# Four whole row tiles in float32, x for two row tiles per step with half-height low terms, and a new order list

## The chip, the core and the metric

The kernel runs on one core of one Trainium2 chip. The metric is the device time of one execution in microseconds (us). The core has five engines with queues of their own that work through their instructions strictly in program order: TensorE (PE, matmuls; PEld is its weight load), VectorE (DVE), ScalarE (ACT), GpSimd (POOL) and SyncE (SP), which issues the DMAs. An instruction that waits holds up everything behind it on its own engine.

## The reference

Linear attention, followed by a two-layer block with a softmax-gated activation:

```python
q_s = softmax(q, over head_dim);  k_s = softmax(k, over the sequence)
kv  = einsum('bhsd,bhse->bhde', k_s, v)          # 8 batches, 8 heads, seq 576, head_dim 64
x   = einsum('bhsd,bhde->bhse', q_s, kv)         # as 4608 rows of 512
h   = x @ w_in                                   # 512 -> 1024
solu = h * softmax(h, over the 1024)
out = ((solu - mean) / sqrt(var + 1e-6) * g_ln) @ w_out      # 1024 -> 512
```

All inputs and outputs are float32; q is drawn with a spread of 0.8.

## The kernel before

The 4608 rows are 36 row tiles of 128. A batch b has four tiles (b, 0) to (b, 3); the 64 rows that are left of two neighbouring batches make one further tile (b, 4) of the odd batch, the "rest tile". For each tile there are three works: x (attention product, transposed), h (the first big matmul with the activation behind it) and o (the second big matmul and the store). Besides there are K and V (per batch: keys, values, the kv product), Q and R (softmax of q and its transpose, R for the rest tiles), S (scales), w and y (weights from HBM), W and Z (weights scaled into float16 pairs) and P (four idle matmuls on the zeroed tile bd2).

Float32 products are made in float16 as high and low parts. For h, each tile takes 24 matmuls of 128x128 by 512 columns (L605); for o, 24 more (L679). For x (`attend`, L573), a head's kv is a block of 64 columns, and rows 0 to 63 and 64 to 127 hold the high and the low part of q: one matmul of all 128 rows with kv-high in both halves, one with kv-low above zeros. Two heads write the two column halves of a result at the same time, so these matmuls are 128 rows by 64 columns. One tile takes 16 of them at 128 columns; a rest tile takes 32 at 64 columns, 16 per batch.

The first tiles are done in float32 ("whole", WHOLE = 2 tiles): q is transposed on PE (`whole_queries`, L511), x is made by `attend_whole` (L551) and h by eight float32 matmuls (L597) with the unscaled weights iw. Their order of weight blocks is FIRST = 3, 0, 2, 1. Whole tiles need neither the float16 weights wi nor the float16 kv (tile bd).

Buffers matter in three places. PSUM holds two h results, one o result (a second kind of bank is used for some of the last six tiles), and three banks with the tag "att" that x, kv and the small transposes share. An h result is freed by the Square on ACT (L648) and the low part of u on DVE (L641); an o result by its copy-out, os, on ACT (L689) or DVE (L687).

The order of all of this is written out by hand in the string ORDER: each word names a work, and each occurrence runs that work's generator to its next `yield`. `.v` puts the step on DVE, and no suffix leaves it on its default engine. So ORDER decides what stands behind what on every engine.

Instance names below: h1_1 is the h of batch 1, tile 1; o0_00 is the o of tile (0, 0); os0_00 is its copy-out; e0_3 and u0_3 belong to h0_3; wo is the scaled second weight; gw its unscaled source.

Of the kernel before, what the change touches and what calls it, by code (L numbers as in the profile page):

```python
# [8 lines left out]
F32 = mybir.dt.float32  # L9
# [8 lines left out]
P = 128  # L18

BUFS = 12, 4, 2  # L20
FIRST = 3, 0, 2, 1
WHOLE = 2
ORDER = (
# [76 lines left out]
def linear_attention_solu_ffn(ctx: ExitStack, tc: tile.TileContext, q, k, v, w_in, w_out, g_ln, out):  # L100
# [13 lines left out]
    C = 4  # L114
# [27 lines left out]
    for t in reversed(bd):  # L142
        nc.gpsimd.memset(t, 0.0)
# [291 lines left out]
    def q_softmax(x, parts, n, name, place=None):  # L435
# [30 lines left out]
        if place is not None:  # L466
            return
# [331 lines left out]
```

## Time and profile before

| what | value |
|---|---|
| runs | 468.74, 468.83, 471.92 us |
| median | 468.83 us |
| profiled execution | 472.39 us, of which 470.6 us from first to last instruction |
| PE busy | 443.1 us, 94% |
| DVE busy | 336.1 us, 71% |
| ACT busy | 280.1 us, 60% |
| POOL busy | 212.3 us, 45% |
| mean granted TensorE clock | 0.985 |

The three runs fall apart into two near 468.8 us and one at 471.92 us; the profiled execution lies beside the upper one. TensorE's clock was at its full level (2.4 GHz) but for a few stretches at the lower one (1.2 GHz).

A timeline row reads: start, duration, engine, line, operation, output and inputs, shape, count, and in brackets the idle time of the engine before it with what ended it. A row of merged matmuls counts from the start of the first to the end of the last, and ends overlap with the next start; so the distance between two starts is the better measure of what a stretch cost.

### The profile page before, as it was taken

What the parts mean: (1) busy time and instruction counts of PE and PEld (TensorE: products, weight loads), DVE (VectorE), ACT (ScalarE), POOL (GpSimd) and SP (SyncE); (2) the same over time, 40 slices, a digit from 0 to 9 for tenths busy, and PEclk for the clock granted to TensorE, in tenths of its full rate; (3) what the DMA queues carried; (4) which work ended last, traced back from release to release, by engine and by line L of the source; (5) the groups of instructions that cost most, each with busy time, mean ns of one, the idle gap of its engine ahead of it and who ended that gap; (6) DMA issues with size and microseconds to landing.
All of it is one profiled execution on the core that took longest, in us unless ns stands there. A gap on an engine that the chain in (4) does not pass through costs nothing.

```text
span 470.6 us, 9239 instructions
## 1 busy us (share of the span) xinstructions
PE 443.1 (94%) x3619; PEld 218.2 (46%) x3619; DVE 336.1 (71%) x598; ACT 280.1 (60%) x469; POOL 212.3 (45%) x312
## 2 busy tenths in 40 slices
PE   3579989799999999999999999999999999999996
PEld 0334434255455454544454455444545454444444
DVE  4978999969878897987788857869567654434411
ACT  2858999658458775764765865434766472433320
POOL 3113876547467555832573584233334631212100
PEclk9969999899999999999999999999999999999999
DMA  8889768368976957497876872986422744431432
GB/s 286 289 293 259 194 163 237 71 156 177 240 210 142 232 121 194 118 275 138 221 174 131 205 167 54 229 205 136 116 68 55 118 100 88 68 91 58 99 91 68
DMA packets 139468, 74.53 MB, mean 158 GB/s; under 512 B 116248, under 2 KB 124704, under 8 KB 139424
## 3 DMA queue, kind: packets, MB, share of 16 engines
q1 hardware_dynamic: 139424, 73.94, 63.9%
q8 instruction: 28, 0.46, 0.4%
q14 instruction: 16, 0.13, 0.1%
HBM read 36.70 MB, written 9.44 MB: 98 GB/s over the span
## 4 chain that ended last, share of the span: by engine, by line
PE 83%; DVE 7%; ACT 4%; DMA 3%; issue 2%; SPq 0%; ACTq 0%; DVEq 0%
PE o L679 39%; PE h L605 34%; PE x L573 3%; PE kv L397 3%; PE h L597 2%; DMA w_in<-in_moe_w_in_dram 2%; DMA km<-in_k_dram 1%; DVE top L612 1%; DVE h L634 1%; ACT wo L335 1%; DVE qsum L454 1%; DVE gw L263 1%; DVE qnmx L447 0%; DVE u L641 0%; ACT gw L259 0%
## 5 line engine op out<-in xcount | busy, mean ns | idle before, releaser
L679 PE MATMUL o<-wo,uT 128*128 128x512 f16 (+1 forms) x888 | 199.1, 376 | 3.0 <-ACT os L689 3.0
L605 PE MATMUL h<-wi,xT 128*128 128x512 f16 x816 | 187.9, 379 | 1.6 <-ACT e L648 1.6
L679 PEld LDWEIGHTS <-uT 128*128 128x128 f16 x888 | 86.5, 98 | 101.2 <-issue 5.8
L605 PEld LDWEIGHTS <-xT 128*128 128x128 f16 x816 | 79.1, 98 | 94.3 <-issue 2.1
L612 DVE TENSOR_REDUCE top<-h 128x1 f32<-128x1024 f32 x36 | 43.8, 1218 | 30.9 <-PE h L605 30.1
L641 DVE SCALAR_TENSOR_TENSOR u<-h,nmu,u 128x1024 f16<-128x1024 f32 x36 | 45.9, 1275 | 17.1 <-ACT u L639 16.9
L634 DVE SCALAR_TENSOR_TENSOR h<-h,ph,e 128x1024 f32<-128x1024 f32 x36 | 46.2, 1284 | 10.3 <-POOL ph L631 7.2
L648 ACT ACTIVATE e<-h,nmu 128x1024 f32<-128x1024 f32 x36 | 40.0, 1110 | 17.5 <-DVE u L641 17.3
L628 POOL TENSOR_TENSOR p<-pi,mone 128x1 f32<-128x1 f32 x36 | 23.9, 665 | 45.9 <-DVE pi L625 43.8
L614 ACT ACTIVATE nm<-top,hs 128x1 f32<-128x1 f32 x30 | 8.8, 294 | 56.7 <-DVE top L612 56.7
L639 ACT ACTIVATE u<-h,nmu 128x1024 f16<-128x1024 f32 x36 | 40.0, 1111 | 0.9
L461 POOL TENSOR_TENSOR qm<-qm,qrec 128x1024 f32<-128x1024 f32 x14 | 26.6, 1902 | 24.8 <-DVE qrec L458 13.6
L618 ACT ACTIVATE e<-h,nm,hs 128x1024 f32<-128x1024 f32 x30 | 36.0, 1201 | 0.7
L689 ACT ACTIVATE os<-o,rr 128x512 f32<-128x512 f32 (+1 forms) x25 | 16.8, 674 | 30.0 <-PE o L679 23.4
L383 POOL TENSOR_TENSOR km<-km,kb 128x1152 f32<-128x1152 f32 x11 | 29.0, 2641 | 7.1 <-ACT kb L361 7.1
L471 POOL TENSOR_TENSOR qhl<-qm,qhl 128x1024 f16<-128x1024 f32 x10 | 21.3, 2130 | 23.5 <-ACT qhl L160 13.5
L636 ACT ACTIVATE nmu<-s 128x1 f32<-128x1 f32 x36 | 7.3, 203 | 41.1 <-DVE h L634 39.0
L622 POOL TENSOR_SCALAR am<-nm 128x1 f32<-128x1 f32 x22 | 10.2, 462 | 45.7 <-ACT nm L614 45.6
L449 POOL TENSOR_TENSOR qm<-qm,qnmx 128x1024 f32<-128x1024 f32 (+1 forms) x15 | 26.8, 1786 | 8.6 <-DVE qnmx L447 8.5
L661 POOL TENSOR_TENSOR r<-var,mhalf 128x1 f32<-128x1 f32 x36 | 19.7, 552 | 23.5 <-DVE var L658 21.4
L582 DVE SCALAR_TENSOR_TENSOR xT<-x,xT 128x512 f16<-128x512 f32 x34 | 22.8, 679 | 8.6 <-ACT xT L580 8.6
L580 ACT ACTIVATE xT<-x 128x512 f16<-128x512 f32 x34 | 19.4, 591 | 7.6 <-PE x L573 7.6
(147 smaller groups left out, 536.9 us busy)
## 6 DMA issues: line engine op xcount, KB each, us to landing
v<-in_v_dram SPq DMA_DIRECT2D x32, 288.0 KB, 4.1
km<-in_k_dram SPq DMA_DIRECT2D x7, 1152.0 KB, 6.9
out_dram<-os SPq DMA_DIRECT2D x31, 256.0 KB, 2.9
qm<-in_q_dram SPq DMA_DIRECT2D x7, 1024.0 KB, 6.1
w_in<-in_moe_w_in_dram SPq DMA_DIRECT2D x8, 512.0 KB, 8.2
w_out<-in_moe_w_out_dram SPq DMA_DIRECT2D x8, 512.0 KB, 6.1
out_dram<-os SPq DMA_DIRECT2D x10, 128.0 KB, 2.4
km<-in_k_dram SPq DMA_DIRECT2D x2, 576.0 KB, 6.7
```

The source lines that it names most:

```text
L383: on(nc.gpsimd).tensor_tensor(km[:, ns], km[:, ns], wide, op=ALU.subtract)
L449: on(nc.gpsimd).tensor_tensor(x, x, wide(nmx), op=ALU.add)
L461: on(nc.gpsimd).tensor_tensor(x, x, wide(rec), op=ALU.mult)
L605: nc.tensor.matmul(h[:, ns], xT[:, t, kc], wi[:, s, kc, ns], start=(i == 0), stop=(i == len(terms) - 1))
L612: nc.vector.tensor_reduce(top, h, axis=AX.X, op=ALU.max, negate=True)
L618: nc.scalar.activation(e, h, AF.Exp, bias=nm, scale=hs, accum_out=z)
L628: nc.gpsimd.tensor_tensor(p, pi, mone, op=ALU.pow)
L634: nc.vector.scalar_tensor_tensor(h, h, ph, e, op0=ALU.mult, op1=ALU.mult, accum_out=s1)
L639: nc.scalar.activation(u[:, 0], h, AF.Identity, bias=nmu)
L641: nc.vector.scalar_tensor_tensor(u[:, 1], h, nmu, u[:, 0], op0=ALU.add, op1=ALU.subtract)
L648: nc.scalar.activation(e, h, AF.Square, bias=nmu, accum_out=s2)
L679: nc.tensor.matmul(o, uT[:, j, f], wo[:, s, f, cols], start=(f == 0 and j == 0 and s == 0), stop=(f == NF - 1 and j == 1))
```

## The change

Whole tiles. WHOLE goes from 2 to 4, so all four full tiles of batch 0 run in float32 from q to h. `whole_queries` now takes a range of tiles: tiles 2 and 3 share one softmax, and each has its own transposes on PE. Their DMA transpose and their split into high and low parts are gone.

x for two tiles. From batch 1 on, one x step makes a pair of tiles, so its matmuls have 256 columns. For the upper four heads the places of q's high and low part are swapped. The low part of kv then meets q's high part in rows 0 to 63 for heads 0 to 3 and in rows 64 to 127 for heads 4 to 7, so the low matmuls have 64 rows by 64 columns and the zero halves fall away, with two of the three memsets. The result of a pair lies in two PSUM banks, each copied out on its own. Rest tiles go through the same code with 64 columns.

```diff
-BUFS = 12, 4, 2
+BUFS = 12, 3, 2
-WHOLE = 2
+WHOLE = 4
 ORDER = (
-    "LQ0*2 Q0b LK0 LG Q0c.v V00 K0 Q0c.v LK0 K0 K0.v w3 K0 w3 LG P K0 V02.v Q0b Q0c LG K0 Q0b V00 w0 "
+    "LQ0*2 LK0 Q0a*2 Q0c LK0 K0.v Q0c.v K0 w3 K0.v K0 Q0b Q0a.v w3 K0 V02 Q0a Q0b K0.v Q0a.v Q0c V00 K0.v "
...
-    for t in reversed(bd):
-        nc.gpsimd.memset(t, 0.0)
+    nc.gpsimd.memset(bd[2], 0.0)
...
-                places[0:D, 1, :, i], kvn[hp], s[hp], high[hp], op0=ALU.mult, op1=ALU.subtract
+                places[hp, 1, :, i], kvn[hp], s[hp], high[hp], op0=ALU.mult, op1=ALU.subtract
...
+        parts = [(x[:, hs], hi, lo) for hs, hi, lo in parts()]
+        for y, hi, lo in parts:
+            cast(on(nc.scalar), hi, y)
+        yield
+        for y, hi, lo in parts:
+            on(nc.gpsimd).tensor_tensor(lo, y, hi, op=ALU.subtract)
...
-    def attend(row_tile):
+    def attend(row_tiles):
...
-            for pr in range(NP):
-                for s in range(2):
-                    for j in range(2):
-                        nc.tensor.matmul(
-                            acc[j * D : (j + 1) * D, pr, cols], t[:, s, 2 * pr + j], qT[:, 2 * pr + j, cols],
-                            start=(s == 0), stop=(s == 1),
-                        )
+            for s, g, i in turns:
+                rows = slice(g * D, (g + 1) * D) if s else slice(0, P)
+                for j in range(2):
+                    head = g * H // 2 + 2 * i + j
+                    nc.tensor.matmul(
+                        accs[g][j * D : (j + 1) * D, i, :, cols], t[rows, s, head], qT[rows, :, head, cols],
+                        start=(m == s == i == 0), stop=(m + 1 == len(groups) and s == 1 and 2 * i + 2 == NP),
+                    )
...
-        nc.scalar.activation(xT[:, 0], acc, AF.Copy, scale=1.0 / QS)
-        yield
-        nc.vector.scalar_tensor_tensor(xT[:, 1], acc, 1.0 / QS, xT[:, 0], op0=ALU.mult, op1=ALU.subtract)
-        yield
+        for acc, ns in zip(accs, halves):
+            nc.scalar.activation(xT[:, 0, ns], acc, AF.Copy, scale=1.0 / QS)
+            yield
+            nc.vector.scalar_tensor_tensor(xT[:, 1, ns], acc, 1.0 / QS, xT[:, 0, ns], op0=ALU.mult, op1=ALU.subtract)
+            yield
...
-        works[f"Q{b}c"] = queries(b, 2, 4)
+        works[f"Q{b}c"] = whole_queries(b, 2, 4) if (b, 3) in whole else queries(b, 2, 4)
```

ORDER is a new list throughout. Three places of it are shown. The first is PE where the first o result ends and the next one begins. Before, o0_10 follows o0_00 directly:

```order
L679 MATMUL o0_00_947<-wo_68,uT0_0_538 128x512
L679 LDWEIGHTS uT0_1_729
L679 MATMUL o0_10_1021<-wo_68,uT0_1_729 128x512
L679 LDWEIGHTS uT0_1_729
L679 MATMUL o0_10_1021<-wo_68,uT0_1_729 128x512
```

In the change the last third of h1_1 stands there (eight matmuls in all), and o0_10 comes after it:

```order
L694 MATMUL o0_00_863<-wo_68,uT0_0_527 128x512
L620 LDWEIGHTS xT1_0_814
L620 MATMUL h1_1_841<-wi_67,xT1_0_814 128x512
L620 LDWEIGHTS xT1_0_814
L620 MATMUL h1_1_841<-wi_67,xT1_0_814 128x512
```

The 24 matmuls of h1_1 stood ahead of o0_00 as one block; in the change they are three blocks of eight, ahead of, inside and behind o0_00.

The second place is ACT at the copy-out of the first o result. Before, from the last scaled weights on:

```order
L335 ACTIVATE wo_68<-gw3_750,gs_882 128x512 x2
L618 ACTIVATE e0_3_954,z0_3_955<-h0_3_771,nm0_3_896,hs0_456 128x1024
L451 ACTIVATE qm1_446<-qm1_446 128x8x128
L451 ACTIVATE qr0_450<-qr0_450 128x512
L636 ACTIVATE nmu0_3_986<-s10_3_984 128x1
L160 COPY vm_78<-v2_0_799 128x9x64
L639 ACTIVATE u0_3_990<-h0_3_771,nmu0_3_986 128x1024
L614 ACTIVATE nm1_1_1008<-top1_1_1006,hs1_805 128x1
L689 ACTIVATE os0_00_1014<-o0_00_947,rr0_0_941 128x512
```

In the change:

```order
L335 ACTIVATE wo_68<-gw3_567,gs_783 128x512 x2
L451 ACTIVATE qm1_485<-qm1_485 128x8x128
L633 ACTIVATE e0_3_871,z0_3_872<-h0_3_729,nm0_3_832,one_75 128x1024
L704 ACTIVATE os0_00_917<-o0_00_863,rr0_0_816 128x512
L651 ACTIVATE nmu0_3_923<-s10_3_921 128x1
L654 ACTIVATE u0_3_925<-h0_3_729,nmu0_3_923 128x1024
```

The copy-out moved from behind nm1_1, u0_3 and nmu0_3 to right behind e0_3.

The third place is ACT around the Square (s2) of tile (0, 2), which frees the PSUM room of h1_1. Before:

```order
L636 ACTIVATE nmu0_2_783<-s10_2_781 128x1
L639 ACTIVATE u0_2_786<-h0_2_610,nmu0_2_783 128x1024
L313 ACTIVATE junk_out3_810,gw_sum_94<-gw3_750 128x1024
L580 ACTIVATE xT1_1_860<-x1_1_826 128x512
L648 ACTIVATE e0_2_721,s20_2_873<-h0_2_610,nmu0_2_783 128x1024
L580 ACTIVATE xT1_0_884<-x1_0_843 128x512
L335 ACTIVATE wo_68<-gw0_428,gs_882 128x512
```

In the change:

```order
L654 ACTIVATE u0_2_766<-h0_2_552,nmu0_2_753 128x1024
L428 COPY bd1_81<-bd1_81 64x256
L335 ACTIVATE wo_68<-gw0_445,gs_783 128x512
L335 ACTIVATE wo_68<-gw0_445,gs_783 128x512
L595 ACTIVATE xT1_0_814<-x1_0_0_787 128x512
L663 ACTIVATE e0_2_709,s20_2_822<-h0_2_552,nmu0_2_753 128x1024
L595 ACTIVATE xT1_0_814<-x1_0_1_788 128x512
```

Two of the eight scalings of wo moved ahead of that Square, and the last of the weight sums (junk_out) lies further ahead than the rows shown.

## Rows read from the trace of the kernel before

**Rows 1.** The page's first part: busy time, share of span, instructions.

```profile
PE 443.1 (94%) x3619; PEld 218.2 (46%) x3619; DVE 336.1 (71%) x598; ACT 280.1 (60%) x469; POOL 212.3 (45%) x312
```

**Rows 2.** Windows: stretch, its length, PE, PEld, DVE, ACT, POOL busy, clock, DMA.

```profile
80.00:90.00 10.00, 7.01 (x29) 2.79 (x26) 9.71 (x16) 8.82 (x16) 3.10 (x5) 0.88 0.22 65
90.00:100.00 10.00, 10.00 (x45) 4.45 (x44) 5.40 (x13) 3.16 (x5) 4.60 (x5) 0.95 0.93 216
...
40.00:90.00 50.00, 43.50 (x359) 20.43 (x357) 47.51 (x79) 46.71 (x78) 33.04 (x39) 0.98 0.69 178
90.00:460.00 370.00, 369.02 (x2986) 181.32 (x2985) 258.87 (x457) 209.75 (x357) 168.45 (x259) 1.00 0.63 144
```

**Rows 3.** Chain that ended last, in order of time: start, us, what.

```profile
37.25 5.17 PE h L597 x12
...
438.41 28.57 PE o L679 x156
```

**Rows 4.** Timeline of PE, 60 to 95 us.

```profile
74.05 5.34 PE L605 MATMUL h<-wi,xT 128*128 128x512 f16 x24 [0.29 <-ACT e L648]
79.23 5.34 PE L679 MATMUL o<-wo,uT 128*128 128x512 f16 x24
87.56 7.03 PE L679 MATMUL o<-wo,uT 128*128 128x512 f16 x24 [2.98 <-ACT os L689]
```

**Rows 5.** Timeline of ACT, 60 to 95 us.

```profile
72.80 1.11 ACT L648 ACTIVATE e<-h,nmu 128x1024 f32<-128x1024 f32 x1
...
78.83 2.56 ACT L335 ACTIVATE wo<-gw,gs 128x512 f16<-128x512 f32 x4
81.29 1.19 ACT L618 ACTIVATE e<-h,nm,hs 128x1024 f32<-128x1024 f32 x1
...
86.63 0.29 ACT L614 ACTIVATE nm<-top,hs 128x1 f32<-128x1 f32 x1 [0.87 <-DVE top L612]
86.83 0.67 ACT L689 ACTIVATE os<-o,rr 128x512 f32<-128x512 f32 x1
```

**Rows 6.** Lines by form: xcount, busy us, mean ns, idle before.

```profile
L597 PE MATMUL h<-iw,xT 128*128 128x512 f32 x32 | 15.5, 632 | 0.0
...
L580 ACT ACTIVATE xT<-x 128x512 f16<-128x512 f32 x34 | 19.4, 591 | 7.6 <-PE x L573 7.6
L160 ACT CAST qhl<-qm 128x1024 f16<-128x1024 f32 x8 | 8.3, 1036 | 1.1 <-POOL qm L461 1.1
L160 ACT COPY qT<-qt 128x512 f32<-128x512 f32 x2 | 1.1, 564 | 0.0
L166 ACT ACTIVATE xT<-x 128x256 f32<-128x256 f32 x2 | 0.7, 374 | 0.0
```

**Rows 7.** Timeline of PE, 24 to 60 us, at the first scale.

```profile
34.07 3.08 PE L597 MATMUL h<-iw,xT 128*128 128x512 f32 x4
36.98 0.27 PE L172 MATMUL wide_in<-ident,m_in 128*128 128x128 f32 x1
```

**Rows 8.** Timeline of ACT, 24 to 48 us, the scale's first use.

```profile
38.19 2.19 ACT L288 ACTIVATE wi<-iw,s_in 128x1024 f16<-128x1024 f32 x2 [1.25 <-DVE isc L285]
```

**Rows 9.** Timelines of PE at three x steps.

```profile
128.43 1.08 PE L573 MATMUL x<-qT,bd 128*64 128x128 f16 x32
129.34 0.67 PE L573 MATMUL x<-qTr,bd 128*64 128x64 f16 x32
129.95 0.60 PE L679 MATMUL o<-wo,uT 128*128 128x512 f16 x2
...
184.85 1.08 PE L573 MATMUL x<-qT,bd 128*64 128x128 f16 x32
185.87 0.82 PE L679 MATMUL o<-wo,uT 128*128 128x512 f16 x3
...
290.06 0.70 PE L573 MATMUL x<-qTr,bd 128*64 128x64 f16 x32
290.69 2.03 PE L397 MATMUL kv<-vm,km 64*64 64x65 f32 x122
```

More of the change, by code (lines that the diff above doesn't have):

```diff
@@ L459, in q_softmax @@
         yield
-        if place is None:
-            on(nc.gpsimd).tensor_tensor(x, x, wide(rec), op=ALU.mult)
-        else:
-            y, z = (a.rearrange("p (i n) d -> p i n d", i=2) for a in (x, wide(rec)))
-            on(nc.gpsimd).tensor_tensor(place, y, z, op=ALU.mult)
+        if places is not None:
+            for i, place in enumerate(places):
+                y, z = (a if len(shape) == 3 else a[:, :, i] for a in (x, wide(rec)))
+                y, z, place = (a.rearrange(e + " d -> p i n d", i=2) for a, e in ((y, "p (i n)"), (z, "p (i n)"), (place, "p (n i)")))
+                on(nc.gpsimd).tensor_tensor(place, y, z, op=ALU.mult)
+                yield
+            return
+        on(nc.gpsimd).tensor_tensor(x, x, wide(rec), op=ALU.mult)
         yield
-        if place is not None:
-            return
-        hi, lo = parts()
-        cast(on(nc.scalar), hi, x)
+        parts = [(x[:, hs], hi, lo) for hs, hi, lo in parts()]
+        for y, hi, lo in parts:
+            cast(on(nc.scalar), hi, y)
         yield
-        on(nc.gpsimd).tensor_tensor(lo, x, hi, op=ALU.subtract)
+        for y, hi, lo in parts:
+            on(nc.gpsimd).tensor_tensor(lo, y, hi, op=ALU.subtract)
         yield
     qT_of, hl_of = {}, {}
+    QUARTERS = slice(0, H // 2), slice(H // 2, H)
     def queries(b, c0, c1):
@@ L485, in parts @@
             hl = hl_of[b, c0 // 2]
-            if n == 1:
-                return (hl[:, c0 % 2, :, i] for i in range(2))
-            return (hl[:, :, :, i].rearrange("p c h d -> p h c d") for i in range(2))
+            for g, hs in enumerate(QUARTERS):
+                if n == 1:
+                    yield hs, *(hl[:, c0 % 2, hs, i ^ g] for i in range(2))
+                else:
+                    yield hs, *(hl[:, :, hs, i ^ g].rearrange("p c h d -> p h c d") for i in range(2))
         yield from q_softmax(x[:, :, 0] if n == 1 else x, parts, H * n, f"{b}_{c0}")
@@ L498, in queries, with whole_queries @@
         )
-    def whole_queries(b, c):
-        first = c // 2 * 2
+    def whole_queries(b, c0, c1):
+        first = c0 // 2 * 2
         if ("whole", first) not in hl_of:
             hl_of["whole", first] = sb.tile([P, 2, H, D], F32, name=f"qn{b}_{first}", tag="qhl", bufs=1)
-        qn = hl_of["whole", first][:, c % 2]
-        place = qn.rearrange("p (n i) d -> p i n d", i=2)
-        yield from q_softmax(raw["qm"][:, :, c], None, H, f"{b}_{c}", place)
-        flat = qn.rearrange("p h d -> p (h d)")
-        turned = ps.tile([P, NP, P], F32, name=f"qt{b}_{c}", tag="att", bufs=3)
-        for i in range(NP):
-            nc.tensor.transpose(turned[:, i], flat[:, i * P : (i + 1) * P], ident)
-        yield
-        if (b, c) not in qT_of:
-            t = sb.tile([P, 2, NP, P], F32, name=f"qT{b}_{first}", tag="qT", bufs=2)
-            qT_of.update({(b, k): t for k in (first, first + 1) if (b, k) in whole})
-        cast(on(nc.scalar), qT_of[b, c][:, c % 2], turned)
+        cs = range(c0, c1)
+        qn = [hl_of["whole", first][:, c % 2] for c in cs]
+        x = raw["qm"][:, :, c0:c1]
+        yield from q_softmax(x[:, :, 0] if len(cs) == 1 else x, None, H * len(cs), f"{b}_{c0}", qn)
+        for c, y in zip(cs, qn):
+            flat = y.rearrange("p h d -> p (h d)")
+            turned = ps.tile([P, NP, P], F32, name=f"qt{b}_{c}", tag="att", bufs=3)
+            for i in range(NP):
+                nc.tensor.transpose(turned[:, i], flat[:, i * P : (i + 1) * P], ident)
+            yield
+            if (b, c) not in qT_of:
+                t = sb.tile([P, 2, NP, P], F32, name=f"qT{b}_{first}", tag="qT", bufs=2)
+                qT_of.update({(b, k): t for k in (first, first + 1) if (b, k) in whole})
+            cast(on(nc.scalar), qT_of[b, c][:, c % 2], turned)
+            yield
     def rest_queries(b):
@@ L520, in parts @@
             hl_of["rest"] = sb.tile([P, H, 2, D], F16, name=f"qhlr{b}", tag="qhlr", bufs=1)
-            return (hl_of["rest"][:, :, i] for i in range(2))
+            for g, hs in enumerate(QUARTERS):
+                yield hs, *(hl_of["rest"][:, hs, i ^ g] for i in range(2))
         yield from q_softmax(raw["qr"], parts, H, f"r{b}")
@@ L556, in attend_whole @@
             yield
-    def attend(row_tile):
-        b, c = row_tile
+    def attend(row_tiles):
+        (b, c), n = row_tiles[0], len(row_tiles)
         name = f"{b}_{c}"
         if c < C:
-            groups = [(b, qT_of[b, c][:, c % 2], slice(0, P))]
+            groups = [(b, qT_of[b, c][:, c % 2 : c % 2 + n], slice(0, P))]
         else:
-            groups = [(b - 1 + j, qT_of["rest", b // 2], slice(j * R, (j + 1) * R)) for j in range(2)]
-        acc = ps.tile([P, NP, P], F32, name=f"x{name}", tag="att", bufs=3)
-        for bb, qT, cols in groups:
-            t = kv_of[bb][0]
-            for pr in range(NP):
-                for s in range(2):
-                    for j in range(2):
-                        nc.tensor.matmul(
-                            acc[j * D : (j + 1) * D, pr, cols], t[:, s, 2 * pr + j], qT[:, 2 * pr + j, cols],
-                            start=(s == 0), stop=(s == 1),
-                        )
-        yield
-        xT = sb.tile([P, 2, NP, P], F16, name=f"xT{name}", tag="xT", bufs=XB)
-        xT_of[row_tile] = xT
-        nc.scalar.activation(xT[:, 0], acc, AF.Copy, scale=1.0 / QS)
-        yield
-        nc.vector.scalar_tensor_tensor(xT[:, 1], acc, 1.0 / QS, xT[:, 0], op0=ALU.mult, op1=ALU.subtract)
-        yield
@@ new lines, in attend @@
+            groups = [(b - 1 + j, qT_of["rest", b // 2].unsqueeze(1), slice(j * R, (j + 1) * R)) for j in range(2)]
+        flat = [ps.tile([P, 512], F32, name=f"x{name}_{g}", tag="att", bufs=3) for g in range(2)]
+        accs = [t[:, 0 : NP // 2 * n * P].rearrange("p (i c k) -> p i c k", c=n, k=P) for t in flat]
+        turns = [(0, g, i) for g in range(2) for i in range(NP // 2)] + [(1, g, i) for i in range(NP // 2) for g in range(2)]
+        for m, (bb, qT, cols) in enumerate(groups):
+            t = kv_of[bb][0]
+            for s, g, i in turns:
[6 more added lines that the diff above has]
+                    )
@@ new lines, in attend @@
+        yield
+        halves = [slice(g * NP // 2, (g + 1) * NP // 2) for g in range(2)]
+        xT = sb.tile([P, 2, NP, n, P], F16, name=f"xT{name}", tag="xT", bufs=XB)
+        for r, row_tile in enumerate(row_tiles):
+            xT_of[row_tile] = xT[:, :, :, r]
+        for acc, ns in zip(accs, halves):
+            nc.scalar.activation(xT[:, 0, ns], acc, AF.Copy, scale=1.0 / QS)
+            yield
+            nc.vector.scalar_tensor_tensor(xT[:, 1, ns], acc, 1.0 / QS, xT[:, 0, ns], op0=ALU.mult, op1=ALU.subtract)
+            yield
@@ L707, in linear_attention_solu_ffn @@
     whole = tiles[:WHOLE]
+    firsts = [[t] for t in tiles[:4]] + [[(b, c), (b, c + 1)] for b in range(1, B) for c in (0, 2)] + [[(b, C)] for b in range(1, B, 2)]
     works = {}
@@ L741, in linear_attention_solu_ffn @@
     for t, row_tile in enumerate(tiles):
-        works[f"x{t}"] = attend_whole(*row_tile) if row_tile in whole else attend(row_tile)
         works[f"h{t}"] = hidden(row_tile)
         works[f"o{t}"] = project(row_tile)
+    for group in firsts:
+        works[f"x{tiles.index(group[0])}"] = attend_whole(*group[0]) if group[0] in whole else attend(group)
     for b in range(B):
```

4 lines of the change are left out of this document (2 added, 2 removed), and 143 rows, old and new, of the table ORDER.

## The prediction

> **What bounds the kernel now.** I read the page's busy times first, then windows by stage, then the chain that ended last, then the timelines of PE and ACT at the one place where PE stands still for long. PE is busy for 443.1 of 470.6 us [rows 1], but what that is worth depends on the stage. From 90 to 460 us PE is busy for 369.02 of 370.00 us while DVE is busy for 70% and ACT for 57% of it: there only PE's own work counts, and all but 0.98 us of it is back to back. Between 40 and 90 us it is the other way round: DVE is busy for 47.51 and ACT for 46.71 of 50 us, PE for 43.50, with idle matmuls (P) among that [rows 2]. There the weights are scaled, the keys prepared and the first five h results worked off, and PE waits for ACT and DVE. So the time is: the moment when PE's unbroken stretch begins, plus PE's work from there, plus a tail. PE's last 156 matmuls end at 466.98 us [rows 3]; copy-out and store bring the span to 470.6, launch and end the execution to 472.39.
>
> That unbroken stretch begins with a stumble. o0_00 runs from 79.23; then PE stands still for 2.98 us until ACT has copied it out, since there is one PSUM bank for o results, and o0_10 starts at 87.56 and takes 7.03 us [rows 4]. The same 24 matmuls cost 5.18 us where PE is at full clock (24 x 0.216, from the 5.34 us of the rows above less the end of the last one). The granted clock falls to the lower level (1.2 GHz) at the idle stretch: its mean is 0.88 from 80 to 90 us and 0.95 from 90 to 100 [rows 2]. That costs 1.85 us more. On ACT the copy-out stood behind nm1_1, which waited for DVE [rows 5]. So o0_00 had ended at about 84.5, and its copy-out began at 86.83.
>
> **A, the beginning of the unbroken stretch.** In the change, eight matmuls of h1_1 lie between o0_00 and o0_10, and the copy-out stands right behind e0_3. What must be there first is h1_1's PSUM room, freed by the Square of tile (0, 2): before, it ran from 72.80 to about 74.0, and h1_1 began at 74.05 [rows 5, 4]. Ahead of this Square ACT now has two more copies of qT (2 x 0.56), one 512 wide and seven 256 wide x copy-outs in place of three and two (7 x 0.37 + 0.59 - 2 x 0.37 - 3 x 0.59 = +0.67), and two scalings of wo (2 x 0.64); the casts of q are halved in size and doubled in number, about even [rows 5, 6]. That is 3.1 us by durations, some 2 us by starts, since on ACT neighbours overlap by about 0.1 us. Against it, ACT's wait of 1.25 us for the first scale [rows 8] should go: PE's transpose wide_in stood behind float32 matmuls of h0_0 that ran at half clock (3.08 us for four records, against 0.43 each) and waited for the last block of w_in [rows 7]; in the change only blocks 3 and 0, which come earlier, stand ahead of it. The DMA transpose of qT for tiles 2 and 3 goes too, so the weights behind it on SP's queue are issued sooner; ACT is the bound there, so this earns nothing by itself. The Square then ends between 74.7 and 77.0; I take 75.7, near the small end, because the removed wait is certain and the overlap is what ACT's rows show throughout.
>
> From there PE has 24 matmuls of h1_1 and 24 of o0_00, 2 x 5.18 = 10.36 us, so o0_10 starts at 86.1 (85.1 to 87.4) instead of 87.56. Two conditions: wo's last quarter must be there about 7.4 us after the Square (8 x 0.216 + 6 x 0.216 + 8 x 0.216 + 12 x 0.216), at 83.1, and on ACT it ended at 81.39 before; and the copy-out (0.67) must fit under the last eight of h1_1 (1.73 us), which it does if e0_3 ends by 84.4 (82.5 before, 81.29 + 1.19). **A = -1.5 us (-2.4 to 0).** At this point both kernels have done the same h and o work.
>
> The two more float32 tiles are paid ahead of that point. A float32 matmul of h leaves two records (32 for two tiles, [rows 6]), 5.17 us for twelve of them [rows 3], so eight matmuls cost 6.90 us against 5.18 in float16: 3.45 us for two tiles. It lies under ACT and DVE, which are full in these 50 us; without that cover it is 3.45 us more. The two memsets, the smaller x buffers (three double ones in place of four), the halved casts and the extra copy-outs of the rest tiles lie on POOL, ACT and DVE beside PE's bound stage, at nothing; if ACT or DVE were full there, they would be a few tenths of a us per batch.
>
> **B, the clock.** With no idle stretch before o0_10 its 24 matmuls take 5.18 us: **B = -1.85 us** in this execution.
>
> **C, the x steps.** Two tiles take 1.02 us to the next matmul when it is 128 wide (184.85 to 185.87), and 0.91 when it is again 64 wide (128.43 to 129.34) [rows 9]. So 16 couples of 128 columns take 0.91, 57 ns each, and the change of width afterwards 0.11. A rest tile takes 0.61 to the next wide matmul, so 0.50 for 16 couples of 64 columns; 0.63 when 64x64 matmuls of kv follow [rows 9]: that change of width costs as much. The kv step shows what four quarters do: 122 records in 2.03 us, about 60 ns for four of them, where one float32 record of 65 columns alone is 5.17/12 x 65/512 = 0.055 us [rows 3, 9]. So four run together. A pair in the change is four couples of 256 columns (4 x 0.108, half of 0.216), two foursomes at 0.108, and one change of width more: 0.43 + 0.22 + 0.11 = 0.76 against 0.91, -0.15 us for each of 13 pairs in the unbroken stretch, -2.0. A rest tile goes from wide to narrow and back for each of its two batches: 0.25 + 0.13 to 0.25 + 3 x 0.11 = 0.71 to 0.83 against 0.50, and its step stands alone more often, 17 steps where there were 14, each with one change of width on the way out (0.11) and a like one on the way in: 4 x 0.27 + 3 x 0.22 = +1.7. **C = -0.3 us.** Bounds: if a change between the two narrow forms were free, -0.26 a pair (-3.4), rest tiles about even and 0.66 for the three more steps, -2.7; if the quarters did not overlap, +0.06 a pair, +2.5 in all.
>
> The Trainium skill's page TensorEngine Tiling (Array Packing), section Tiling Modes, says that a change of tiling mode drains TensorE, where a change of tile does not. The 0.11 and 0.13 us of rows 9 agree with that, and the rule is what speaks against this change: without it C would be its low bound.
>
> **D.** o5_30 now follows o5_20 with only a rest step between (some 0.9 us for a copy-out of 0.67 and its waits): +0.2 (0 to 0.4). The 0.98 us of idle in rows 2 may stay or go; I count nothing.
>
> **The sum.** 472.39 - 1.5 - 1.85 - 0.3 + 0.2 = 468.9 us, against the profiled execution's own time. That execution lies 3.56 us above the median of the runs shown and beside the highest, 471.92. What sets such executions apart isn't shown; a half clock behind the stumble or before 40 us, present in one and absent in another, is the nearest candidate, and then B is nothing, or little, in the two runs near 468.8. From the median without B: 468.83 - 1.6 = 467.2; with all of B 465.4. I take **467.3 us**, since the two low runs are the majority.
>
> **The rivals.** First, *the packing pays in full*: changes between narrow forms cost nothing, C is -2.7, A comes to its low end and part of B is real: 468.83 - 2.7 - 2.4 - 0.5 = 463.2. For it: quarters do run together in kv. Against: both narrow changes in rows 9 cost a tenth. The page TensorE: Matmul & The Clock Gate, Part 3 (Measured speedup vs the span model), would have it so: matmuls on different tiles take one matmul's time and some 4 ns per tile. Chance 0.20. Second, *a new wait in the early stage* (slower): on PE x1_0 now stands ahead of the last two float32 matmuls of h0_3, and x1_0 needs kv of batch 1 and a DMA transpose; if these come late, h0_3, e0_3, the copy-out and o0_10 all slip, and an idle stretch of 3 us brings the half clock again (1.85). It decides from about 4.5 us late on; at 5: 468.83 - 1.6 + 5 + 1.85 = 474.1. For it: everything in 40 to 90 us is packed. Against: q of batch 1 is loaded sooner. Chance 0.12. Third, *the cover is gone*: the float32 tiles are not hidden and add their 3.45: 470.7, as if nothing had been gained. Chance 0.10. The forecast, a gain of 0 to 4 us, has 0.58.
>
> **How the numbers follow.** Within 1% (about what a measurement of this kernel can tell from no change) is 464.1 to 473.5: the forecast and the third rival, 0.68. Faster by over 1%: the first rival, 0.20. Slower: the second, 0.12. The range runs from 463.5 to 472.0 and leaves out the low half of the first rival and most of the second.
>
> **What would show it.** In the changed profile: no wait of PE for os behind o0_00, and o0_10 in 5.2 to 5.4 us (A, B); o0_10 starting at 85 to 87.5; wide_in before 36 us; 0.87 us from a pair's first x matmul to a wide one (0.76 plus the change out), 0.8 to 0.95 for a rest tile (C): 0.76 for a pair says the first rival, over 1.0 that quarters don't overlap; PE busy for 99% of the unbroken stretch. Wrong would be idle stretches of PE over 1 us behind 90 us, a second half clock, or o0_10 after 88.

## The result

The changed kernel takes 464.76 us (median of 7 runs, 464.32 to 465.42) against 468.83 of the kernel before (median of 7 runs, 467.68 to 471.92): a ratio of 0.989, 95% interval 0.986 to 0.992. That is 4.1 us less by the medians: just over the gain of 0 to 4 us of the forecast, inside what I had called within 1% (464.1), and 2.5 us under the 467.3 I had predicted. The profiled execution took 464.6 us, with a span of 462.8. One execution of before among those timed later (481.95 us, mean granted clock 0.951) was in a slower state of the chip and is left out of the counts of executions below.

The stretch that [rows 2] showed of before, now of the changed kernel. Windows: stretch, its length, PE, PEld, DVE, ACT, POOL busy (with counts), clock, DMA share, GB/s.

```profile
40.00:72.00 32.00, 29.52 (x259) 13.55 (x258) 30.70 (x56) 31.64 (x55) 19.97 (x21) 1.00 0.68 175
80.00:90.00 10.00, 10.00 (x49) 4.66 (x47) 9.78 (x17) 7.33 (x13) 5.68 (x10) 1.00 0.56 131
85.00:95.00 10.00, 10.00 (x49) 4.75 (x47) 8.82 (x17) 6.51 (x13) 5.67 (x9) 1.00 1.00 229
90.00:450.00 360.00, 360.00 (x2740) 171.93 (x2738) 257.82 (x475) 212.41 (x371) 164.00 (x257) 1.00 0.64 144
```

PE is busy for all of 360 us behind 90, where it was busy for 369.02 of 370, and the granted clock is 1.00 (2.4 GHz) from 80 us on, where it was 0.88 from 80 to 90. The timeline of PE at the place of [rows 4]:

```profile
72.53 1.89 PE L620 MATMUL h<-wi,xT 128*128 128x512 f16 x8 [0.27 <-ACT e L663]
74.25 1.46 PE L694 MATMUL o<-wo,uT 128*128 128x512 f16 x6
...
81.16 1.89 PE L620 MATMUL h<-wi,xT 128*128 128x512 f16 x8
82.88 5.34 PE L694 MATMUL o<-wo,uT 128*128 128x512 f16 x24
88.06 1.89 PE L620 MATMUL h<-wi,xT 128*128 128x512 f16 x8
```

And of ACT, at that of [rows 5]:

```profile
71.28 1.10 ACT L663 ACTIVATE e<-h,nmu 128x1024 f32<-128x1024 f32 x1
...
78.26 1.19 ACT L633 ACTIVATE e<-h,nm,one 128x1024 f32<-128x1024 f32 x1
...
81.36 0.69 ACT L704 ACTIVATE os<-o,rr 128x512 f32<-128x512 f32 x1 [1.82 <-PE o L694]
```

The Square of tile (0, 2) starts at 71.28 (before 72.80). o0_10 starts at 82.88 (before 87.56), and its 24 matmuls take 5.18 us to the next start (before 6.86). ACT is now waiting for o0_00 when it ends, not PE for ACT.

By these marks the two profiles differ by 7.8 us of span: 4.68 up to o0_10, 1.68 in its matmuls, 1.18 from there to PE's last matmul, 0.26 in the tail. That is almost twice what the medians differ by. So the first question was how much of it belongs to the change, and how much to the one execution of before that was profiled.

### The profile page after: what moved, and what is told of

The parts are those of the page before. It is cut to its first block, busy times and chain, and to the rows that moved or that the text cites. A ratio compares the mean times of both kernels' runs of the same rounds, so it can differ in the third digit from the quotient of the medians.

```text
span 462.8 us, 8794 instructions
## 1 busy us (share of the span) xinstructions
PE 439.2 (95%) x3379; PEld 212.9 (46%) x3379; DVE 339.3 (73%) x622; ACT 285.2 (62%) x492; POOL 202.6 (44%) x308
## 4 chain that ended last, share of the span: by engine, by line
PE 86%; ACT 7%; DVE 3%; DMA 1%; issue 1%; SPq 0%; ACTq 0%
PE o L694 41%; PE h L620 36%; PE kv L397 4%; PE x L585 3%; DMA km<-in_k_dram 1%; ACT gw L259 1%; ACT e L633 1%; PE h L612 1%; ACT km L385 1%; ACT wi L288 1%; ACT junk_out L313 1%; PE warm_up L751 1%; PE wide L358 1%; DVE iw L263 1%; ACT e L663 1%
## 5 line engine op out<-in xcount | busy, mean ns | idle before, releaser
L620 PE MATMUL h<-wi,xT 128*128 128x512 f16 x768 | 178.0, 379 | 0.3 <-ACT e L663 0.3
L620 PEld LDWEIGHTS <-xT 128*128 128x128 f16 x768 | 74.3, 98 | 88.2 <-issue 1.8
L704 ACT ACTIVATE os<-o,rr 128x512 f32<-128x512 f32 (+1 forms) x21 | 14.2, 674 | 30.2 <-PE o L694 22.9
L449 POOL TENSOR_TENSOR qm<-qm,qnmx 128x1024 f32<-128x1024 f32 (+1 forms) x12 | 21.1, 1770 | 20.6 <-DVE qnmx L447 20.5
L612 PE MATMUL h<-iw,xT 128*128 128x512 f32 x64 | 29.5, 599 | 0.1
L467 POOL TENSOR_TENSOR qm<-qm,qrec 128x1024 f32<-128x1024 f32 x12 | 23.0, 1920 | 11.7 <-DVE qrec L458 5.4
L383 POOL TENSOR_TENSOR km<-km,kb 128x1152 f32<-128x1152 f32 x10 | 26.3, 2632 | 3.4 <-ACT kb L361 3.2
L597 DVE SCALAR_TENSOR_TENSOR xT<-x,xT 128x512 f16<-128x512 f32 (+1 forms) x36 | 22.3, 623 | 7.2 <-ACT xT L595 7.1
L702 DVE TENSOR_SCALAR os<-o,rr 128x512 f32<-128x512 f32 (+1 forms) x16 | 11.6, 728 | 20.6 <-PE o L694 15.3
L474 POOL TENSOR_TENSOR qhl<-qm,qhl 128x512 f16<-128x512 f32 x20 | 24.1, 1228 | 5.3 <-ACT qhl L160 5.1
```

Source lines behind the costliest of these rows:

```text
L383: on(nc.gpsimd).tensor_tensor(km[:, ns], km[:, ns], wide, op=ALU.subtract)
L474: on(nc.gpsimd).tensor_tensor(lo, y, hi, op=ALU.subtract)
L612: nc.tensor.matmul(h[:, ns], xT[:, kc], iw[kc][:, ns], start=(i == 0), stop=(i == NP - 1))
L620: nc.tensor.matmul(h[:, ns], xT[:, t, kc], wi[:, s, kc, ns], start=(i == 0), stop=(i == len(terms) - 1))
```

## What is in question

Theory: the gain is the stall in front of o0_10 and the half clock behind it; the packed x, the float32 tiles and the rest of the order roughly cancel. Rivals: the packed x brings it (the prediction's first rival); or an earlier start of the early stage does, as the two profiles side by side suggest.

## Experiments

**1. The kernel before, again, and its early stage.** Two runs: the kernel unchanged, and the kernel with the first x copy-outs taken out from behind the conversion of the last block of w_in:

```diff
-K0 w1 P x0 w2 LK1 w2 w1 x1 V12 w1*2 Q0c x0.v K1.v
+K0 x0 P x0.v w1 w2 LK1 w2 w1 x1 V12 w1*2 Q0c K1.v
```

> The kernel before, once more, to see in which place its executions differ: the three runs shown fall apart into two near 468.8 us and one at 471.92, and the profile belongs to the upper group (472.39). Theory 1 (the clock): the upper executions hold half clock that the lower ones don't, so the mean granted clock stands near 0.985 in runs of some 471.8 us and nearer to 1 in runs of some 468.7, and in a lower execution the 24 matmuls of o0_10 take near 5.3 us. Theory 2 (the early stage): what differs lies ahead of 40 us (a transfer that lands later), the half clock behind o0_00 is in all of them, and o0_10 takes some 7 us in the lower ones too but starts some 3 us sooner than at 87.56.

> The kernel before with one thing moved: both copy-outs of the first x (tile (0, 0)) stand ahead of the conversion of the last block of w_in, on ACT and on DVE. In the profile of before that conversion holds ACT for 3.99 us until its transfer lands, and the first copy-out stands behind it. Theory (that wait is what makes the early stage of before late): PE's h0_0 begins at about 30 instead of 34 us, no half clock ahead of 40 us, the wait of ACT for isc (1.25 us) goes, o0_10 starts 1 to 3 us sooner, 466 to 468 us in all. Rival (the stretch from 40 to 90 us is full of work of ACT and DVE that does not depend on it): o0_10 starts within 0.5 us of the kernel before and the time is the same.

Unchanged: 468.13 us, ratio 0.9998 to before (0.9965 to 1.003), profiled at 467.88. With the copy-outs moved: 468.75, ratio 1.0005 (0.9977 to 1.0033). PE's timeline at the stall in the second profile of before:

```profile
74.53 5.34 PE L679 MATMUL o<-wo,uT 128*128 128x512 f16 x24
82.85 6.91 PE L679 MATMUL o<-wo,uT 128*128 128x512 f16 x24 [2.97 <-ACT os L689]
89.60 5.34 PE L605 MATMUL h<-wi,xT 128*128 128x512 f16 x24
```

The same place with the copy-outs moved:

```profile
83.67 8.22 PE L679 MATMUL o<-wo,uT 128*128 128x512 f16 x24 [2.98 <-ACT os L689]
91.72 5.34 PE L605 MATMUL h<-wi,xT 128*128 128x512 f16 x24
```

And ACT's rows of the last w_in block and of the Square of tile (0, 2) in the second profile of before:

```profile
26.80 1.16 ACT L259 ACTIVATE iw<-w_in 128x1024 f32<-128x1024 f32 x1 [0.98 <-DMA w_in<-in_moe_w_in_dram]
...
68.10 1.11 ACT L648 ACTIVATE e<-h,nmu 128x1024 f32<-128x1024 f32 x1
```

In the first profile the row of the w_in block starts at 29.88, behind a wait of 3.99 us:

```profile
29.88 1.12 ACT L259 ACTIVATE iw<-w_in 128x1024 f32<-128x1024 f32 x1 [3.99 <-DMA w_in<-in_moe_w_in_dram]
```

PE ran at the lower clock for a while in both: until about 37 us in the first (granted clock 0.50 from 30 to 35 us), earlier in the second (0.61 from 12 to 25 us).

So one block of w_in landed 3 us later in the first profile, and everything up to o0_00 came 4.7 us later (79.23 against 74.53). That is one execution's; it has nothing to do with the change. That the late block made the whole 4.7 us is argued from these two profiles, not shown. The stall is the same in all three profiles (2.98, 2.97 and 2.98 us), but what its 24 matmuls take behind it is not: 6.86, 6.75 and 8.05 us to the next start, against 5.18 at full clock.

Of the first expectation, theory 2 holds for the two profiles of before: the early stage moved by 4.7 us, and the lower clock behind o0_00 is in the ordinary execution too. Theory 1 holds in so far as executions without any lower clock are shorter: of 40 executions of before timed beside these, 34 had a mean granted clock under 0.998 and took 466.06 to 471.97 us (median 468.36), and six had 0.999 or more and took 465.82 to 467.54 (median 466.5). With those timed beside the later experiments it is 70 and 16 executions, with medians of 468.57 and 466.74. The difference, 1.8 us, is about what step B priced. But the mean doesn't tell where the clock was low: the profile of experiment 5 has a mean of 0.993 and its lower clock between 10 and 30 us, not behind o0_00. So 34 of the 40 is the most that can have B.

The moved copy-outs brought h0_0 to 28.99 us (30.33 without the edit), but wide_in stayed at 32.08 (32.15), o0_10 came at 83.67 (82.85), and the time is the same: the rival holds. In an ordinary execution the place of these copy-outs is not what makes the stretch behind late. Whether moving them would help an execution with the late block, no run shows.

**2. The copy-out alone, both ways.** In before it is moved ahead of u0_3 and nm1_1 on ACT, with PE's order untouched; in the changed kernel it is put back behind them.

```diff
 (before)
-Z R1.v o0 h3.v h2 V20 h3 Q1c.v o0.v h2.v h5 Q1c o2.v h3.v o0 V22.v*2
+Z R1.v o0 h3.v h2 V20 o0.v o0 h3 Q1c.v h2.v h5 Q1c o2.v h3.v V22.v*2
 (changed)
-LQ1 o0 h2 h3 o0 h2.v o0 h3*3 h5.v h1.v S0 V20 Q1c.v o0.v K2.v ... V22 h3 h5.v K2
+LQ1 o0 h2 h3 o0 h2.v h3*3 h5.v h1.v S0 V20 Q1c.v K2.v ... V22 h3 h5.v o0 o0.v K2
```

> The kernel before with one thing moved: the copy-out of o0_00 stands ahead of u0_3 and nm1_1 on ACT instead of behind them; PE's order is untouched. Theory (steps A and B of the prediction): the copy-out runs at about 84.7 instead of 86.83, PE's stall of 2.98 us shrinks to 0.8 to 1.0 us, o0_10 starts some 2.1 us sooner and its 24 matmuls take 5.2 to 5.4 us if a stall of that length leaves the clock up: 2.1 to 4 us faster. Rival (the h results behind are the bound, so that a sooner o0_10 only waits later): the stall comes back in front of the next h, and the time is within 0.5 us of before.

> The changed kernel with the copy-out of o0_00 put back on ACT to where it stood before, behind u0_3, the Square of tile (0, 3) and nm1_1. Theory (A and B): PE stands still in front of o0_10 for 3.5 to 4 us, the granted clock falls behind it, o0_10 starts at about 86.7 and takes some 7 us: 5 to 6 us slower than the changed kernel, about 470. Rival (the gain lies elsewhere): less than 2 us slower.

Before with the copy-out moved: 464.87 us, 3.35 less than the 468.22 of before beside it (ratio 0.9933, 0.9904 to 0.9963). Changed with it put back: 471.97, 7.2 more than the changed kernel. PE's timelines at o0_10, first of the former, then of the latter:

```profile
75.74 5.34 PE L679 MATMUL o<-wo,uT 128*128 128x512 f16 x24
81.92 5.34 PE L679 MATMUL o<-wo,uT 128*128 128x512 f16 x24 [0.84 <-ACT os L689]
```

```profile
80.75 1.89 PE L620 MATMUL h<-wi,xT 128*128 128x512 f16 x8
86.92 7.85 PE L694 MATMUL o<-wo,uT 128*128 128x512 f16 x24 [4.29 <-ACT os L704]
```

Behind the stall of 0.84 us the clock stays up; behind the one of 4.29 us it is 0.76 from 80 to 90 us, and the 24 matmuls take 7.69 us to the next start. Stall and clock together are 4.3 + 2.5 = 6.8 of the 7.2 us; in the two profiled executions (464.6 and 471.12 us) o0_10 starts 4.04 us later and takes 2.51 us longer, which is all of their 6.5 us. And one instruction's place on ACT, in the kernel before, gives the time of the whole change within the noise (464.87 and 464.76 us; the intervals of the two ratios overlap).

**3. The packed x.** Three edits. First, x for pairs alone, put into before with the moved copy-out (ORDER of before, both tiles at the place of the first):

```diff
-ORDER = (...)   # of the change
+ORDER = (...)   # of before, copy-out moved
-WHOLE = 4
+WHOLE = 2
...
+        gen = attend(group)          # both tiles' words drive one generator
+        for t in group:
+            works[f"x{tiles.index(t)}"] = gen
```

> The kernel before with the copy-out of o0_00 moved (as in b_os), and with one part of the change added: x made for two tiles per step with half-height low terms, in the order of before (both tiles at the place of the first; a few copy-outs follow at once). Two tiles in float32 as before. Compared with b_os. Theory (step C: the gains and costs of the packed x nearly cancel): 0.9 us from a pair's first matmul to the next wide one against 1.02 for two tiles, 0.86 for a rest tile against 0.5 to 0.6, together within 1 us of b_os, 464 to 466. Rival 1 (the packing is what made the changed kernel faster): 2 to 3 us faster than b_os. Rival 2 (copy-outs in halves and later x steps make PE wait in the order of before): PE idle more than 1 us behind 90 us, slower.

485.99 us: slower by 21 than the same without pairs. The waits of PE behind 88 us:

```profile
PE x L587 <- DVE xT L600: 5.9, 5, 1.4
PE h L623 <- ACT e L666: 3.6, 3, 1.9
PE kv L399 <- DVE xT L600: 2.7, 1, 2.7
...
```

That is rival 2: a pair needs two of the three "att" banks at once, and in the order of before the next x or kv follows before they are copied out. With two smaller waits (1.4 and 1.2 us) these make 14.8 of the 21 us; the rest is not broken down. (Three pairs and two rest tiles run all their steps at the first word here, the others at the words of their two tiles in turn.) The run says nothing of C's own size; it shows that pairs, placed like this, need another order around them.

Second, low terms of full height again in the changed kernel; third, in a rest step all high terms first:

```diff
-    nc.gpsimd.memset(bd[2], 0.0)
+    for t in reversed(bd):
+        nc.gpsimd.memset(t, 0.0)
...
-                rows = slice(g * D, (g + 1) * D) if s else slice(0, P)
+                rows = slice(0, P)
```

```diff
-        for m, (bb, qT, cols) in enumerate(groups):
...
-            for s, g, i in turns:
+        for part in range(2):
+            for m, (bb, qT, cols), (s, g, i) in [(m, gr, tu) for m, gr in enumerate(groups) for tu in turns if tu[0] == part]:
...
```

> The changed kernel with low terms of full height again, on zeroed halves (three memsets as before); pairs of tiles and their order stay. Theory (packing four quarters saves half the low terms' time and pays for it with a change of form): a pair goes from 0.902 to about 0.95 us (8 couples of 0.108 and the change out), a rest step from 0.863 to about 0.60; 14 x 0.05 - 4 x 0.26 = -0.4 us, 464.4 in all. Rival (packing pays in full): a pair at 1.1 us or more, 2 us slower or more.

> The changed kernel with one thing re-ordered inside a rest step: the high terms of both batches come first, then the low terms of both, so that the step changes between full and half height once instead of three times. Theory (a change of form costs 0.09 to 0.13 us each, as rows 9 show for width): a rest step goes from 0.863 us to about 0.66, four of them save 0.8 us, 464.0 in all. Rival (what a rest step costs more than before is the half-height matmuls themselves): the step stays at 0.8 to 0.86 us, and the time too.

Full height: 465.20 us (464.35 to 465.54). High terms first: 464.00 (463.59 to 464.58; ratio to before 0.9895, 0.9859 to 0.9931). PE's rows at one pair and one rest step, each with the row behind it, of the changed kernel, of full height, and a rest step of high terms first:

```profile
119.27 0.97 PE L585 MATMUL x<-qT,bd 128*64 128x256 f16 x16
120.17 4.06 PE L694 MATMUL o<-wo,uT 128*128 128x512 f16 x18
124.16 0.93 PE L585 MATMUL x<-qTr,bd 128*64 128x64 f16 x32
125.02 2.76 PE L620 MATMUL h<-wi,xT 128*128 128x512 f16 x12
```

```profile
118.37 1.06 PE L586 MATMUL x<-qT,bd 128*64 128x256 f16 x16
119.37 4.06 PE L695 MATMUL o<-wo,uT 128*128 128x512 f16 x18
123.36 0.69 PE L586 MATMUL x<-qTr,bd 128*64 128x64 f16 x32
123.98 2.33 PE L621 MATMUL h<-wi,xT 128*128 128x512 f16 x10
```

```profile
123.89 0.69 PE L585 MATMUL x<-qTr,bd 128*64 128x64 f16 x32
124.51 1.68 PE L620 MATMUL h<-wi,xT 128*128 128x512 f16 x7
```

From the first matmul to the next row a pair takes 0.90 us packed and 1.00 at full height. A rest step takes 0.86 packed, 0.62 at full height, and 0.62 packed with two changes between full and half height fewer. So such a change of form costs 0.12 us here, as the expectation had it from [rows 9]. The Trainium skill's page TensorEngine Tiling (Array Packing), section Tiling Modes, has a change of mode drain TensorE: the 0.12 us agree. With it, halving the low terms of a pair earns 0.10 us instead of the 0.22 that it would if the change were free, which was the first rival. The fourth rest step, at 374 us, takes about 0.90 us in all three, and there it is not the matmuls: it stands alone between two o results, which need the same PSUM bank. In the changed kernel its own 0.89 us cover the copy-out (374.58 to 375.27) to within 0.05 us; where the step is shorter PE waits for the rest, in the version with high terms first as in the one of full height:

```profile
PE o L694 <- ACT os L704: 0.2, 1, 0.2
```

That is what step D of the prediction priced. Full height came out 0.8 us above the 464.4 that I had expected, at the edge of what four runs tell; I had its pair at 0.95 instead of 1.00.

**4. The float32 tiles and the cover.** In the changed kernel the first block of h0_2 and of h0_3 is multiplied twice (3.45 us more on PE); or the last four groups of P are left out (3.5 us less); or tiles (0, 2) and (0, 3) go back to float16.

```diff
+                    for once in (True, False) if i == 0 and row_tile[1] > 1 else (False,):
-                    nc.tensor.matmul(h[:, ns], xT[:, kc], iw[kc][:, ns], start=(i == 0), stop=(i == NP - 1))
+                        nc.tensor.matmul(h[:, ns], xT[:, kc], iw[kc][:, ns], start=(i == 0), stop=once or i == NP - 1)
```

```diff
-h1 P y1 y3 ... V11.v W P y2 ... y0 P h3 ... h2 P Z
+h1 y1 y3 ... V11.v W y2 ... y0 h3 ... h2 Z
```

```diff
-WHOLE = 4
+WHOLE = 2
...
-x3 h2 Q1c
+x3 S0 W h2 Q1c
...
```

Not shown of the last: a K0 and the last W also stand sooner, x of these two tiles makes both halves of its copy-out in one step, and h of batch 0 advances by three terms per word instead of two.

> The changed kernel with more float32 work on PE: the first block of weights of h0_2 and of h0_3 is multiplied twice (the first result is overwritten), two more float32 matmuls for each, 3.45 us in all, which is what the two further float32 tiles cost PE. Theory (they lie under ACT and DVE): o0_10 starts within 0.7 us of the changed kernel, the time is within 1 us of 464.8. Rival (the cover is gone: PE bounds that stage): o0_10 starts 2.5 to 3.5 us later, 467 to 468.

> The changed kernel without the last four groups of idle matmuls (P; 16 matmuls, 3.5 us of PE between 47 and 69 us). Theory (PE sets the stretch from 50 to 72 us): the Square of tile (0, 2) and o0_10 come 1 to 2.5 us sooner, 462.5 to 463.7 us in all. Rival (ACT or DVE sets it): PE only waits for longer, the time within 0.5 us of 464.8; if the idle stretches get long, the granted clock falls and the time rises.

> The changed kernel with two instead of four tiles in float32: tiles (0, 2) and (0, 3) go back to float16 (q split, transposed by DMA, x from bd, h in 24 float16 matmuls); the rest of the change stays, and the words of the order that this needs (scales, the last of wi and bd) stand a little sooner. Theory (what the run with more float32 matmuls says: PE, not ACT or DVE, sets the stretch from 50 to 72 us, so the two further float32 tiles cost most of their 3.45 us there): the Square of tile (0, 2) ends 2 to 3 us sooner, o0_10 starts at 80 to 81 instead of 82.88, some 462.5 us in all. Rival (ACT sets that stretch, as the prediction had it): o0_10 starts at 82.5 to 83.5, the time within 0.7 us of 464.8; or later, if the moved words make DVE wait.

More float32: 467.65 us, 2.9 more than the changed kernel; o0_10 starts at 85.12. Without P: 464.67, no change. The window of 40 to 72 us with more float32, and PE's waits without P (in total, times, longest):

```profile
40.00:72.00 32.00, 30.21 (x256) 14.02 (x254) 27.42 (x52) 29.00 (x50) 19.40 (x21) 1.00 0.65 161
```

```profile
PE h L612 <- ACT e L663: 2.7, 2, 1.5
...
PE x L585 <- ACT bd L428: 1.4, 1, 1.4
```

The two runs belong together, and in each the rival of its expectation holds (for more float32 by the time; o0_10 moved a little less than its 2.5 to 3.5 us). Take 3.5 us of PE work away, and PE only waits longer for ACT's Squares and bd: ACT (31.64 of 32 us) sets the stretch, and so the 3.45 us of the float32 tiles lie under it as the prediction had it. Add as much, and o0_10 comes 2.24 us later, with ACT and DVE now waiting (29.00 and 27.42 us busy): the cover is nearly used up, and at most 1.2 us of it were left.

Back in float16: 475.90 us. That is no price of float16 by itself. In this order the transpose of q stands on SP ahead of the loads of w_out, which are issued at 38.42 instead of 30.43 us. ACT waits for them, PE behind it for bd, and the granted clock is 0.76 from 40 to 75 us:

```profile
ACT gw L259 <- DMA w_out<-in_moe_w_out_dram: 5.2, 1, 5.2
```

```profile
48.23 0.78 PE L585 MATMUL x<-qT,bd 128*64 128x128 f16 x12 [6.06 <-ACT bd L428]
```

So whether float16 tiles could be had here at the same time stays open; that this order, as it stands, rests on their transpose being gone is shown.

**5. A pause of PE.** In before PE stands still for about 1 us in the kv step behind the rest step of batch 5, waiting for nothing that the profile shows. I moved that rest step's word in the order:

```diff
-x24 x25 h23 h23.v h21 Q6c.v V70 o18.v x26 h21.v
+x24 x25 h23 x26 h23.v h21 Q6c.v V70 o18.v h21.v
```

> The kernel before with the copy-out of o0_00 moved (as in b_os) and one further thing: the rest tile's x of batches 4 and 5 stands 12 h matmuls sooner, so that it no longer runs straight ahead of the 144 kv matmuls. In every profile of the order of before, PE stands still for 0.8 to 1.1 us inside those kv matmuls and waits for nothing that the profile shows; in the changed kernel, where they are apart, it doesn't. Theory (that pause comes from the two steps of many short instructions standing together, and its going is part of the changed kernel's gain): the pause goes, some 1 us faster than b_os, 463.9. Rival (the pause belongs to the place or the time in the program): it stays.

464.38 us, against 464.87. The edit missed its aim: none of the words passed holds a matmul, so PE's order stayed, the run repeats the kernel of experiment 2, and the pause is there:

```profile
282.17 0.70 PE L573 MATMUL x<-qTr,bd 128*64 128x64 f16 x32
282.80 2.32 PE L397 MATMUL kv<-vm,km 64*64 64x65 f32 x140
285.97 0.33 PE L397 MATMUL kv<-vm,km 64*64 64x65 f32 x4 [0.85 <-issue]
```

It stands behind 140 of 144 records in this profile as in both of before, whether that is at 285, 289 or 293 us, so it belongs to a place in the program. Why there, was not found. The run is worth something all the same: it repeats the time of experiment 2, and its profile has a granted clock of 0.83 from 10 to 30 us where that of experiment 2 has 1.00, yet o0_00 starts at 75.22 against 75.74. So in these two executions a lower clock this early did not make the stretch behind it late.

**6. A better early stage, tried.** High terms first, and around the Square of tile (0, 2):

```diff
-Z*2 K1.v x4 h3 h2 Z h2 h0.v Z x4 o0.v x4 h1.v h2 x4 Z*2 V23
+Z K1.v h3 x4 h2 h2 h0.v h2 x4 o0.v x4 h1.v x4 Z*5 V23
```

> The version a_rest with one place of the early stage re-ordered: on ACT the Square of tile (0, 2) stands directly behind bd, ahead of the x copy-outs and of the first two scalings of wo; on PE the last four float32 matmul records of h0_3 stand ahead of the first pair's x. Theory (ACT's order, not PE's work, sets the start of h1_1, and 1.3 to 1.8 us of ACT's work can stand behind the Square): the Square starts at 69.3 to 69.7 instead of 71.0, h1_1 at 71.0 to 71.5 instead of 72.25, o0_10 at 81.4 to 81.9 instead of 82.6, 463.0 to 463.4 us in all against 464.0. Rival (something else is late there as well: wo, or the low part of xT on DVE): PE waits for wo in o0_00 or for xT in h1_1 instead, and the time stays at 464.

467.01 us, 3 more than without that edit. PE's waits that the version without it does not have:

```profile
PE h L620 <- ACT xT L595: 1.3, 1, 1.3
PE o L694 <- DVE wo L337: 1.1, 1, 1.1
...
PE h L620 <- DVE xT L597: 0.7, 1, 0.7
```

The rival: the Square waited 1.28 us for DVE's low part of u, and wo and xT came late behind it. At this point ACT and DVE are both just in time, and this reordering did not help; whether another would is open. Of the versions tried, high terms first has the lowest median (464.00 against 464.76 and 468.83). The two ratios to before, 0.9895 and 0.9893, don't tell it from the changed kernel; its trace does, by 0.24 us in each of three rest steps.

## Why the prediction came out as it did

The time fell into the range, and the mechanism that I had put the gain on is the one that brought it: stall and clock at o0_10, shown by experiment 2 from both sides. The likeliest value was 2.5 us too high, and that it was no further off is luck in part: of the parts below, A and the uncounted idle miss by over 1 us each in opposite directions.

- **A (-1.5 us).** In the profiled execution it is -4.68, against an ordinary one (experiment 1) it is +0.03: 82.88 and 82.85. By my marks it should have started at 85.1 to 87.4, so this term was wrong. The step from the start of h1_1 to o0_10 was right: 10.36 us predicted, 10.35 from 72.53 to 82.88; in the ordinary execution it is 13.49 (69.36 to 82.85), so the stall of 3 us is gone. The moment of the Square was wrong. Against the ordinary execution it is 3.2 us later (71.28, 68.10), which eats what the stall gives back. My terms gave ACT 2 to 3.1 us more to do ahead of it, and by the two rows below it worked for 2.0 us longer from 20 us on, and was idle for 1.2 us longer. But I subtracted a wait of 1.25 us for isc, the first scale, as certain, and it stood only in the execution with the late block. The row of ACT's 3.99 us for w_in, a little ahead of it in the same timeline, I did not use at all; it was a sign that this execution's early stage was no base for a difference of 1 us. And the 75.7 that I took for the Square's end is not near the small end of my own bounds (74.7 to 77.0), as I wrote, but near their middle.
  The windows from 20 us to the start of that Square, first in the second profile of before, then in the changed kernel (behind the length: PE, PEld, DVE, ACT, POOL):

```profile
20.00:68.10 48.10, 43.51 (x499) 23.20 (x495) 46.65 (x84) 45.51 (x74) 28.73 (x27) 0.95 0.88 249
```

```profile
20.00:71.28 51.28, 47.26 (x479) 24.06 (x480) 47.60 (x92) 47.51 (x81) 22.07 (x23) 1.00 0.77 229
```

- **B (-1.85 us).** The size is about right: 6.86 to 5.18 is 1.68 in the profile that I read (my 1.85 set a row of 7.03 us, which counts the end of the last matmul, against 5.18, which doesn't), 1.57 and 2.87 in the two other profiles with this stall. The step that failed is the choice behind it, that the runs near 468.8 have little or none of it, "since the two low runs are the majority". Both other profiled executions with this stall have it, of 467.88 us and, with the copy-outs moved, of 469.49, and executions of before without any lower clock lie near 466.5. With all of B my own sum said 465.4, which is 0.6 from the result. This choice is the miss that puts the forecast above the result. That the sum with B comes so near is luck in part, with A taken 1.5 us too good and the idle below not counted.
- **C (-0.3 us).** A pair takes 0.90 (0.87 predicted), a rest step 0.86 (0.8 to 0.95). All x steps behind 90 us, each from its first matmul to the next row, take 15.21 us instead of 15.35, and three more steps cost 3 x 0.10 on the way in (in the rows of experiment 3, 18 matmuls take 3.99 us up to the next x, where 18 x 0.216 is 3.89), so C is between +0.1 and +0.2: the 0.03 us by which I had a pair too short, 13 times. The first rival, packing for nothing, is refuted by the 0.12 us of a change of form. (Four quarters of kv took 67 ns by my row, 4 x 2.03/122, and not about 60; that they run together holds.)
- **D (+0.2 us)** is right in its place and came to +0.03: PE has no wait at all behind 90 us, because the rest step there takes as long (0.89 us) as the copy-out needs. With shorter rest steps the 0.2 us appear, as experiment 3 shows.
- **What I counted at nothing:** the 0.98 us of idle in [rows 2] went. It is most of the 1.2 us that PE's unbroken stretch is shorter by, and I had no row to tell that the new order would miss it.
- **Cover of the float32 tiles (0.10 for the third rival):** held, by at most 1.2 us. That the transpose taken off SP "earns nothing by itself" was wrong for this order: with it back, ACT waits 5.2 us for w_out.
- **The second rival** (a new wait early) did not come; nothing in 60 to 72 us makes PE wait longer than 0.62 us. The early stage is later than in the ordinary execution all the same, by more work and more idle time on ACT (A).

Between the second profile of before (467.88 us) and that of the changed kernel (464.6) the whole then reads: +0.03 to o0_10 (+3.17 to the start of h1_1, -3.14 from there), -1.57 in its matmuls (6.75 to 5.18), -1.50 from there to PE's last matmul (pauses of 1.2 us, the rest small differences), -0.26 in the tail, -3.30 in all; by the medians it is -4.1 beside one set of executions of before and -3.5 beside the other (468.22).

## What to carry over

Where one instruction on a slower engine stands between two results of the busiest one, price the stall and the clock behind it first. Here that place alone was worth as much as the whole change: moving one copy-out in the old order gave the same time. A single profile is one execution; before subtracting a wait of it, see whether the runs spread by as much, and whether a transfer that landed late made it. Each change of array form cost 0.11 to 0.13 us here, so sort matmuls by form before cutting their height.

## What was not expected of the hardware

A stall of PE of 0.84 us left the granted clock at its full level. Behind three stalls of the same length (2.97, 2.98 and 2.98 us) it was at the lower one (1.2 GHz) for part of the next 24 matmuls, which took 6.75, 6.86 and 8.05 us instead of 5.18; behind one of 4.29 us they took 7.69. So the same stall cost from 1.6 to 2.9 us afterwards, and the longer one not the most. The same block of w_in landed 3 us apart in two executions of the same program, and in the later one the stage behind it came 4.7 us later.
